# Sigmoid attention and two expert layers on one core: another order for the layer-1 weight work beside attention

## The chip, the core and the metric

The kernel runs on one core of one Trainium2 chip. The metric is device time in microseconds (us) of one execution. Engines are named as in the profile: PE is TensorE (matmuls), PEld its weight loads, DVE VectorE, ACT ScalarE, POOL GpSimd and SP SyncE, which here issues the DMAs.

## What is computed

```
scores = q @ k.T / sqrt(64) - log(448)              # 4 batches, 12 heads, 448 tokens, head size 64
x  = sigmoid(scores) @ v                            # heads side by side: 1792 tokens x 768
h  = x @ w1_in ;  x2 = (h * cos(h)) @ w1_out        # 768 -> 2048 -> 768
h  = x2 @ w2_in
P  = a0 + a1 h + a2 h^2 + a3 h^3
Q  = 1 + |b0| |h| + |b1| h^2
out = (P / (Q + 1e-6)) @ w2_out                     # 768 -> 2048 -> 768
```

The inputs are double precision. The weights reach the chip as pairs of 32-bit words; q, k and v as float32.

## The kernel before

**Products.** A matmul of the expert layers is three f16 products: the scaled operand is split into a high half (`hi`, written by ACT) and the rest (`lo`, written by DVE), and hi*hi, hi*lo and lo*hi are summed. So every weight row block needs a power-of-two scale, which comes from the row's largest magnitude, and every batch of activations needs a scale that comes from a maximum over the batch.

**Attention** fills the first 167 us. It goes by 24 pairs of heads in 84 units `(p, c)`; a unit is one chunk of 128 keys of a pair, and units `(p, None)` take the remaining 64 keys of two pairs together. For a unit, `scores` (L278) writes a tile `s_p_c` in the PSUM pool `pss` (2 tiles), ACT makes the sigmoid `a_p_c` (L280), and `av` (L296) adds its product with v to the PSUM tiles `v_p`. The k and q of a pair are first split into `kh`, `qh` (ACT, L256) and `kl`, `ql` (DVE, L257). When two pairs are complete, `av_out` copies each `v_p` to `raw_p` (ACT, L305) and then takes its maxima into `mx_x` (DVE, L308). The tiles `v_p` come from the PSUM pool `psa` of 4 tiles. All other PSUM tiles of this stage come from the same four: the `px_...` tiles of a maximum over partitions, and the first two products of layer 1, `h0` and `h1`. A tile is handed to the next user in the order in which tiles become free.

**Weight work beside attention.** DVE and ACT prepare layer-1 weights at the same time. There are 18 cells of `w1_in` (row block `r`, column piece `n`) and 2 cells of `w1_out` (`EARLY`). A cell is a load of word pairs `f1i_r_n` or `f1o_f` by SP into one of three buffers (L109), then on DVE `p0` (L78), `p1` (L81), a maximum (L113) and `p2` (L81), which write the value tile `v1i` or `v1o`. Behind a row block, `fin` works out its scale (tiles `re_...`, `s1i`, `i1i`), and then its pieces are split, `hi` on ACT (L343) and `lo` on DVE (L81). The other 14 row blocks of `w1_out` get only their maxima now (`max_cell`): a load `p1o_f` into the same three buffers, and one DVE reduction (L113). Whenever `p2` or such a maximum is through with its buffer, `prefetch` issues the next load of the list.

**Scales of x.** For batch `bt`, `x_begin(bt)` multiplies maxima and weight scales (`mxs_x`), reduces them and spreads the result over a diagonal `dg_x` (three DVE instructions). `xtwo(bt)` is a matmul of ones with it (`px_x`, L101) on PE, and on DVE a reduction `xm_x` and five small instructions that end in the scales `kx_x`. `x_split(0, d)` writes the f16 halves of x for batch 0. `t1_one` and `t1_two` do the same over all scales of `w1_out` (`dg_t`, `px_t`, `rho`, `irho`, `kap`).

**What sets the order.** The instructions of each engine run in the order in which the code emits them. All weight steps and scale steps stand in a list `work`, each with a cost. For every two units `slot()` is called three times; it hands out steps until their cost reaches the same share of the whole as the calls have, and a step with a third element 1 ends the call. The order within the loop is: scores of two units, k and q splits, a slot, `av` of the two units before, `av_out` if due, two slots. After the loop stand `l1_consts(0)`, the 18 matmuls of `h0`, the last `av` and `av_out`, then `h1`. From `h1` on, layer 1 and layer 2 run on PE to the end.

**Before**, `work` is the 20 cells in order with a maximum behind every cell from the fifth on, then batch 0's scale steps and x splits among the last cells, then `t1_one`, two empty steps, `t1_two`, `x_begin(1)`, `x_begin(2)`, `xtwo(1)`, `xtwo(2)`.

## Time and profile before

| | us |
|---|---|
| median of 3 runs | 1055.4 |
| the runs | 1055.65, 1055.4, 1054.65 |
| the profiled execution, its own time | 1054.34 |
| its span in the trace | 1052.4 |
| PE busy | 1030.3 (98%) |
| DVE busy | 806.4 (77%) |
| ACT busy | 575.0 (55%) |
| POOL busy | 212.9 (20%) |

The shares are means over stages with different limits: attention with its weight work lasts to 167.46, where `h1` begins; layer 1 and layer 2 fill the rest. The mean granted TensorE clock over the span is 0.993 of full speed.

### The profile page before, as it was taken

The page shows a single profiled execution, that of the slowest core. Times are in us where ns is not written, and L with a number is a line of the kernel's source. Part 1 is how long each engine was busy: PE and PEld are TensorE (multiplying, and loading weights), DVE is VectorE, ACT ScalarE, POOL GpSimd, SP SyncE. Part 2 cuts the span into 40 slices and gives each one's busy share as a digit, 9 for nine tenths or more (in the row PEclk, how much of TensorE's full clock was granted, in tenths as well). Part 3 has the DMA queues.
Part 4 walks back from the last instruction along what each step waited for, and adds up shares of the span by engine and source line. Part 5 has one row for each costly group of instructions (what it writes and reads, how often), then busy time and mean ns, then how long its engine had stood idle before and what let it go on. Part 6 is the DMA issues. An engine that isn't in the chain of part 4 may idle for free.

```text
span 1052.4 us, 15806 instructions
## 1 busy us (share of the span) xinstructions
PE 1030.3 (98%) x5920; PEld 550.0 (52%) x5920; DVE 806.4 (77%) x1541; ACT 575.0 (55%) x938; POOL 212.9 (20%) x211
## 2 busy tenths in 40 slices
PE   8999899999999999999999998989999999999998
PEld 5444444555555555555555554545565555555665
DVE  5999967877997799869996869888887873887200
ACT  6899886743474327532662555666665653666100
POOL 0000003766242004200240323312221110221000
PEclk9999999999999999999999999999999999999999
DMA  8899813224433562335437330000000000000000
GB/s 290 301 330 338 324 52 106 91 81 140 138 91 111 176 214 81 98 114 159 128 99 284 116 107 1 1 1 9 16 23 16 8 23 16 8 12 13 24 23 31
DMA packets 53485, 110.34 MB, mean 105 GB/s; under 512 B 5280, under 2 KB 29344, under 8 KB 52640
## 3 DMA queue, kind: packets, MB, share of 16 engines
q1 hardware_dynamic: 53408, 109.34, 31.4%
q8 instruction: 46, 0.75, 0.3%
q14 instruction: 31, 0.25, 0.1%
HBM read 91.23 MB, written 18.09 MB: 104 GB/s over the span
## 4 chain that ended last, share of the span: by engine, by line
PE 83%; DVE 8%; ACT 3%; DMA 3%; issue 1%; SPq 0%; DVEq 0%; ACTq 0%
PE hx L539 21%; PE o L614 21%; PE o L920 20%; PE hy L539 16%; PE v L296 3%; PE s L278 2%; DMA f1i<-in_moe_w_in_dram 1%; DVE w L81 1%; DVE t L81 1%; DVE v1i L81 1%; DMA k<-in_k_dram 1%; ACT a L280 1%; DMA f1o<-in_moe_w_out_dram 1%; PE s_None L278 1%; DVE kl L257 1%
## 5 line engine op out<-in xcount | busy, mean ns | idle before, releaser
L539 PEld LDWEIGHTS <-wi 128*128 128x128 f16 x2304 | 226.1, 98 | 212.1 <-issue 4.5
L920 PE MATMUL o<-wo,g 128*128 128x384 f16 (+1 forms) x1536 | 221.9, 326 | 4.1 <-ACT g L143 2.9
L539 PE MATMUL hy<-y,wi 128*128 128x448 f16 x1152 | 224.3, 355 | 0.0
L614 PE MATMUL o<-g,wo 128*128 128x448 f16 x1152 | 220.5, 352 | 0.0
L539 PE MATMUL hx<-x,wi 128*128 128x448 f16 x1152 | 218.7, 352 | 0.2 <-DVE xm_x L102 0.2
L920 PEld LDWEIGHTS <-g 128*128 128x128 f16 (+1 forms) x1536 | 134.2, 101 | 90.2 <-ACT g L143 3.2
L614 PEld LDWEIGHTS <-wo 128*128 128x128 f16 x1152 | 112.7, 98 | 104.3
L78 POOL TENSOR_SCALAR w<-u,aab 128x448 f32<-128x448 f32 x64 | 66.0, 1031 | 334.6 <-ACT u L883 321.2
L588 POOL TENSOR_TENSOR g<-r,g 128x448 f16<-128x448 f32 x64 | 73.1, 1145 | 233.6 <-ACT g L587 230.3
L280 ACT ACTIVATE a<-s,nlogs 128x896 f32<-128x896 f32 x72 | 69.2, 1005 | 16.9 <-PE s L278 16.8
L143 ACT ACTIVATE g<-t,kn 128x448 f16<-128x448 f32 x64 | 42.8, 669 | 54.5 <-DVE t L81 48.1
L894 ACT ACTIVATE u<-w,c 128x448 f32<-128x448 f32 x64 | 42.6, 665 | 52.0 <-DVE w L889 50.5
L81 DVE SCALAR_TENSOR_TENSOR w<-w,c,u 128x448 f32<-128x448 f32 x64 | 43.7, 683 | 31.1 <-ACT u L895 30.3
L575 ACT ACTIVATE k<-hx,quarter,ck 128x448 int32<-128x448 f32 x64 | 45.7, 714 | 36.4 <-PE hx L539 18.9
L78 POOL TENSOR_SCALAR xs<-v1o,s1o 128x384 f32<-128x384 f32 x28 | 26.5, 948 | 188.4 <-DVE v1o L81 186.9
L296 PE MATMUL v<-a,v 128*64 128x448 f32 x288 | 64.2, 560 | 0.0
L883 ACT ACTIVATE u<-hy,i_y 128x448 f32<-128x448 f32 x64 | 39.7, 620 | 36.0 <-PE hy L539 36.0
L887 DVE TENSOR_TENSOR t<-t,h 128x448 f32<-128x448 f32 x64 | 43.8, 685 | 20.2 <-ACT t L885 20.2
L81 DVE SCALAR_TENSOR_TENSOR t<-t,ab,w 128x448 f32<-128x448 f32 x64 | 56.9, 890 | 2.3
L76 DVE TENSOR_SCALAR ob<-o,ig 128x384 f32<-128x384 f32 x12 | 7.4, 614 | 64.4 <-PE o L920 64.4
L81 DVE SCALAR_TENSOR_TENSOR r<-hx,ck,k 128x448 f32<-128x448 f32 x64 | 43.4, 678 | 14.6 <-ACT k L575 14.5
L81 DVE SCALAR_TENSOR_TENSOR r<-hx,kap,r 128x448 f32<-128x448 f32 x64 | 43.3, 677 | 10.2 <-ACT r L581 10.0
(157 smaller groups left out, 1273.0 us busy)
## 6 DMA issues: line engine op xcount, KB each, us to landing
f2o<-in_moe_w_out_dram SPq DMA_DIRECT2D x32, 384.0 KB, 3.3
p1o<-in_moe_w_out_dram SPq DMA_DIRECT2D x14, 768.0 KB, 5.7
f1o<-in_moe_w_out_dram SPq DMA_DIRECT2D x28, 384.0 KB, 3.4
f1i<-in_moe_w_in_dram SPq DMA_DIRECT2D x12, 768.0 KB, 6.8
f2i<-in_moe_w_in_dram SPq DMA_DIRECT2D x24, 384.0 KB, 3.4
k<-in_k_dram SPq DMA_DIRECT2D x24, 256.0 KB, 4.9
wso<-hlo SPq DMA_DIRECT2D x32, 192.0 KB, 2.3
wi<-wsi SPq DMA_DIRECT2D x6, 1024.0 KB, 10.7
```

The source lines that it names most:

```text
L78: eng.tensor_scalar(out=o, in0=i, scalar1=s1, scalar2=s2, op0=op0, op1=op1)
L81: eng.scalar_tensor_tensor(out=o, in0=i0, scalar=s, in1=i1, op0=op0, op1=op1)
L143: A.activation(out=hi, in_=x, func=AF.Copy, scale=s)
L280: A.activation(out=t, in_=ps[:, :, :S], func=AF.Sigmoid, bias=cst["nlogs"], scale=QK)
L296: T.matmul(pvt[2 * o + j][h * D:(h + 1) * D, :S], vt[r, b * D:(b + 1) * D], at[r, x], start=c == (None if i else 0), stop=c == (NC - 1 if ...
L539: T.matmul(ps[:, :S], w[:, wl, f * P:(f + 1) * P], x[:, xl, :], start=(n == 0), stop=(n == 3 * ND - 1),)
L575: A.activation(out=kk, in_=ps[:, :S], func=AF.Identity, scale=ck, bias=cst["quarter"])
L588: G.tensor_tensor(out=g[:, 1, :], in0=r, in1=g[:, 0, :], op=ALU.subtract)
L614: T.matmul(acc[e][:, :S], w[:, wl, e * P:(e + 1) * P], g[:, gl, :], start=(f == 0 and i == 0), stop=(f == NF - 1 and i == 2),)
L887: V.tensor_tensor(out=t, in0=t, in1=h, op=ALU.mult)
L894: A.activation(out=u, in_=w, func=AF.Abs_reciprocal_sqrt, bias=cst["c1"])
L920: T.matmul(ps[o:o + m, :HALF], gt[bt, f][:, gl, c0:c0 + m], wo[f][:, wl, n0:n0 + HALF], start=(n == 0), stop=(n == 3 * NF - 1),)
```

## The change

The steps are the same, and each engine has as many instructions as before; their order is another.

- At the start one load of weights is issued ahead of the first parameters instead of three; the second follows k and q of pair 2, the third the second v.
- In the 18 cells of `w1_in`, a maximum of `w1_out` follows only every second cell from the eighth on (6 of 14). The other 8 stand in a list of 13 last steps, one behind each as long as there are any.
- Those last steps hold the scale steps of batches 0, 1 and 2 and the six x splits, in the order of `tail`; a step that is due brings a cell or a split of weights with it. `xtwo(0)` now comes three entries after `x_begin(0)`.
- `t1_two` and `l1_consts(0)` stand behind `h0` and the last `av_out`, ahead of `h1`.
- `kx` has three buffers instead of two.

```diff
--- before.py
+++ after.py
@@ -153,7 +153,7 @@
     SEAM = 2
     ESPLIT = 3
     NW = 3
-    WN, XN = 2, 7
+    XM, XN = 6, 7
     W_IN = [(c0, HALF) for c0 in range(0, 4 * HALF, HALF)] + [(4 * HALF, 256), (4 * HALF + 256, 256)]
     W_OUT = pieces(DM, HALF)
     W_BIG = [(0, DM), (DM, DM), (2 * DM, DFF - 2 * DM)]
@@ -182,7 +182,7 @@
             shr(e, m, 23)
             setexp(s, e, -1.0, 267)
             setexp(i, e, 1.0, -13)
-            kx = col(f"kx_{pfx}{bt}", ND, tag="kx", bufs=2)
+            kx = col(f"kx_{pfx}{bt}", ND, tag="kx", bufs=3)
             ts(V, kx, i_in, s)
             res[bt] = (e, s, i, kx)
 
@@ -414,35 +414,54 @@
             add_w1i(r)
         for f in range(EARLY):
             add_w1o(f)
-        x0 = [(0.5, lambda: x_begin(0)), (0.1, lambda: None), (1.0, lambda: xtwo[0]())]
-        x0 += [(0.75, lambda d=d: x_split(0, d)) for d in range(ND)]
         maxes = [max_cell(f) for f in range(EARLY, NF)]
-        splits = []
-        n_in = ND * len(W_BIG)
-        held = None
-        for n, ((ld, p0, p1, mx, p2), _) in enumerate(cells):
+        splits, held = [], []
+
+        def add_cell(n):
+            (ld, p0, p1, mx, p2), _ = cells[n]
             loads.append(ld)
-            work += [p0, held, p1, mx, p2] if held else [p0, p1, mx, p2]
-            held = None
+            work.extend([p0, *held, p1, mx, p2])
+            held.clear()
             if splits:
-                (hi, held), splits = splits[0], splits[1:]
+                hi, lo = splits.pop(0)
                 work.append((0.0, hi))
-            if len(maxes) * (len(cells) - 4) > (NF - EARLY) * (len(cells) - 1 - n):
+                held.append(lo)
+            if n in after:
+                fin, mine = after[n]
+                work.append(fin)
+                splits.extend(cells[i][1] for i in mine)
+
+        def add_max():
+            if maxes:
                 ld, mx = maxes.pop(0)
                 loads.append(ld)
                 work.append(mx)
-            if n in after:
-                fin, mine = after[n]
-                work.append(fin)
-                splits += [cells[i][1] for i in mine]
-            if n >= n_in and x0:
-                for _ in range(3):
-                    if x0:
-                        work.append(x0.pop(0) + (1,))
-        for hi, lo in splits:
-            work += [(0.0, hi), held, (0.0, lambda: None, 1)]
-            held = lo
-        work += [held] + [u + (1,) for u in x0]
+
+        n_in = ND * len(W_BIG)
+        for n in range(n_in):
+            add_cell(n)
+            if n >= XM and n % 2:
+                add_max()
+        xb, xg, xs = (
+            lambda bt: (0.5, lambda: x_begin(bt)), lambda bt: (1.0, lambda: xtwo[bt]()),
+            lambda d: (0.75, lambda: x_split(0, d)),
+        )
+        tail = [xb(0), xb(1), None, xg(0), xs(0), xg(1), xs(1), xs(2), xb(2), xs(3), xs(4), xg(2), xs(5)]
+        nexts = list(range(n_in, len(cells)))
+        for u in tail:
+            if nexts:
+                add_cell(nexts.pop(0))
+            elif splits:
+                hi, lo = splits.pop(0)
+                work.extend([(0.0, hi), *held])
+                held[:] = [lo]
+            else:
+                work.extend(held)
+                held.clear()
+            add_max()
+            if u:
+                work.append(u + (1,))
+        assert not (maxes or splits or held or nexts)
         st1 = {}
 
         def t1_one():
@@ -461,10 +480,7 @@
             ts(V, kap1, i1o, rho)
 
         rho, irho, kap1 = col("rho"), col("irho"), col("kap1", NF)
-        nop = lambda: None
-        work += [(0.7, t1_one, 1), *[(0.1, nop, 1)] * WN, (0.9, t1_two, 1)]
-        work += [(0.5, lambda bt=bt: x_begin(bt), 1) for bt in range(1, B - 1)]
-        work += [(1.0, lambda bt=bt: xtwo[bt](), 1) for bt in range(1, B - 1)]
+        work += [(0.7, t1_one, 1)]
         total = sum(u[0] for u in work)
         SLOTS = 3 * len(units) // 2 - 2
         clock = [0, 0.0]
@@ -485,15 +501,16 @@
             T.matmul(warm[:, :P], ones.to_broadcast([P, P]), ones.to_broadcast([P, P]), start=True, stop=True)
         A.activation(out=ab[:, :1], in_=ones, func=AF.Sigmoid)
         load_v(0)
-        for _ in range(NF64[0]):
-            prefetch()
+        prefetch()
         SY.dma_start(ab[:, 0:4], a.partition_broadcast(P))
         SY.dma_start(ab[:, 4:6], b.partition_broadcast(P))
         steps = prep(0)
         for st in "kh qh kl ql".split():
             steps[st]()
         load_kq(2)
+        prefetch()
         load_v(1)
+        prefetch()
         done = []
         for g in range(0, len(units), 2):
             due = [1] if g == 0 else []
@@ -550,12 +567,13 @@
             V.tensor_tensor(out=iy, in0=i, in1=irho, op=ALU.mult)
             return ck, iy
 
-        L1c = {0: l1_consts(0)}
         h0 = h_matmul("x", 0, 0)
         for p, c in units[-2:]:
             av(p, c)
         av_out(NP - 2)
         av_out(NP - 1)
+        t1_two()
+        L1c = {0: l1_consts(0)}
         h1 = h_matmul("x", 0, 1)
         pa.close()
         bp = ctx.enter_context(tc.tile_pool(name="pb", bufs=1, reuse_waits="tile"))
```

SP's queue from the first weight load on. Each row is one DMA; `f1i_0_1` is the second column piece of row block 0 of `w1_in`, `k_2` the k of pair 2. Before:

```order
L109 DMA f1i_0_0_123<-in_moe_w_in_dram 128x1536
L109 DMA f1i_0_1_125<-in_moe_w_in_dram 128x1536
L109 DMA f1i_0_2_127<-in_moe_w_in_dram 128x1024
L490 DMA ab_87<-in_moe2_a_dram 128x4
L491 DMA ab_87<-in_moe2_b_dram 128x2
L238 DMA k_2_139<-in_k_dram 128x512
L238 DMA q_2_141<-in_q_dram 128x448
L244 DMA v_1_143<-in_v_dram 128x896
```

After:

```order
L109 DMA f1i_0_0_123<-in_moe_w_in_dram 128x1536
L505 DMA ab_87<-in_moe2_a_dram 128x4
L506 DMA ab_87<-in_moe2_b_dram 128x2
L238 DMA k_2_135<-in_k_dram 128x512
L238 DMA q_2_137<-in_q_dram 128x448
L109 DMA f1i_0_1_139<-in_moe_w_in_dram 128x1536
L244 DMA v_1_141<-in_v_dram 128x896
L109 DMA f1i_0_2_143<-in_moe_w_in_dram 128x1024
```

The second and third weight loads moved behind `k_2` and `q_2`, the third behind `v_1` too.

PE's queue around `px_x0`, the matmul with batch 0's maxima. In the names a number behind the tile is its pair and chunk, the last one only a running number. Before:

```order
L278 MATMUL s_19_2_1514<-qh_19_1397,kh_19_1395 128x448 x2
L278 MATMUL s_19_2_1514<-qh_19_1397,kl_19_1396 128x448 x2
L278 MATMUL s_19_2_1514<-ql_19_1398,kh_19_1395 128x448 x2
L101 MATMUL px_x0_1535<-dg_x0_1501,ones_71 128x128
L296 MATMUL v_18_1443<-a_18_None_1463,v_9_1295 64x448
L296 MATMUL v_19_1444<-a_18_None_1463,v_9_1295 64x448
L296 MATMUL v_18_1443<-a_18_None_1463,v_9_1295 64x448
L296 MATMUL v_19_1444<-a_18_None_1463,v_9_1295 64x448
L296 MATMUL v_18_1443<-a_19_0_1472,v_9_1295 64x448
```

After:

```order
L101 MATMUL px_x0_1590<-dg_x0_1418,ones_71 128x128
L278 MATMUL s_20_2_1604<-qh_20_1479,kh_20_1477 128x448 x2
L278 MATMUL s_20_2_1604<-qh_20_1479,kl_20_1478 128x448 x2
L278 MATMUL s_20_2_1604<-ql_20_1480,kh_20_1477 128x448 x2
L278 MATMUL s_20_None_1613<-qh_20_1479,kh_20_1477 128x448
L278 MATMUL s_20_None_1613<-qh_21_1533,kh_21_1531 128x448
L278 MATMUL s_20_None_1613<-qh_20_1479,kl_20_1478 128x448
L278 MATMUL s_20_None_1613<-qh_21_1533,kl_21_1532 128x448
L278 MATMUL s_20_None_1613<-ql_20_1480,kh_20_1477 128x448
L278 MATMUL s_20_None_1613<-ql_21_1534,kh_21_1531 128x448
L296 MATMUL v_20_1630<-a_20_0_1563,v_10_1456 64x448
L296 MATMUL v_21_1631<-a_20_0_1563,v_10_1456 64x448
```

`px_x0` moved behind the last `av` of pair 19 (16 rows later in PE's queue). The second matmul of pair 20's `av`, into `v_21`, comes 11 rows behind it; its PSUM tile was freed by `xm_x0`, the reader of `px_x0`, before; after the change it is the one that the maxima `mx_x3` of `v_18` free.

DVE's queue up to those maxima of `v_18` and `v_19`. Before (`dg_x0`, which `px_x0` reads, stands three rows above the first of these, `m1o<-p1o_15` ten above):

```order
L102 TENSOR_REDUCE xm_x0_1499<-px_x0_1535 128x1
L76 TENSOR_SCALAR xm_x0_1499<-xm_x0_1499 128x1
L76 TENSOR_SCALAR e_x0_1538<-xm_x0_1499 128x1
L78 TENSOR_SCALAR s_x0_1539<-e_x0_1538 128x1
L78 TENSOR_SCALAR i_x0_1540<-e_x0_1538 128x1
L76 TENSOR_SCALAR kx_x0_1545<-i1i_84,s_x0_1539 128x6
L78 TENSOR_SCALAR v1o_1_1553<-f1o_1_1375 128x768
L81 SCALAR_TENSOR_TENSOR wi1_5_1413<-v1i_5_0_1180,s1i_97,wi1_5_1413 128x768
L81 SCALAR_TENSOR_TENSOR v1o_1_1553<-f1o_1_1375,v1o_1_1553 128x768
L113 TENSOR_REDUCE m1o_81<-f1o_1_1375 128x1
L308 TENSOR_REDUCE mx_x3_1582<-v_18_1443 128x1
L308 TENSOR_REDUCE mx_x3_1582<-v_19_1444 128x1
```

After (`dg_x0` stands 14 rows above the first of these, `xm_x0` is the row behind the last):

```order
L113 TENSOR_REDUCE m1o_81<-p1o_9_1369 128x1
L171 TENSOR_TENSOR mxs_x1_1506<-mx_x1_729,i1i_84 128x6
L96 TENSOR_REDUCE pm_x1_1510<-mxs_x1_1506 128x1
L76 TENSOR_SCALAR dg_x1_1509<-ident_66,pm_x1_1510 128x128
L257 TENSOR_TENSOR kl_21_1532<-k_21_1402,kh_21_1531 128x512
L257 TENSOR_TENSOR ql_21_1534<-q_21_1404,qh_21_1533 128x448
L81 SCALAR_TENSOR_TENSOR wi1_5_1299<-v1i_5_1_1175,s1i_97,wi1_5_1299 128x768
L113 TENSOR_REDUCE m1o_81<-p1o_10_1409 128x1
L81 SCALAR_TENSOR_TENSOR wi1_5_1299<-v1i_5_2_1254,s1i_97,wi1_5_1299 128x512
L113 TENSOR_REDUCE m1o_81<-p1o_11_1490 128x1
L308 TENSOR_REDUCE mx_x3_1583<-v_18_1446 128x1
L308 TENSOR_REDUCE mx_x3_1583<-v_19_1447 128x1
```

The maxima of `v_18` have the same number of rows ahead of them. Among these, `p1o_12` to `p1o_15` and the `xm_x0` chain are no longer there; the last `p2` of `v1o_1`, its scale, two `lo` pieces of `wi1_5` and `x_begin(1)` are.

PE's queue between the last `av` and `h1`. Before:

```order
L296 MATMUL v_22_1728<-a_23_1_1792,v_11_1587 64x448
L296 MATMUL v_23_1729<-a_23_1_1792,v_11_1587 64x448
L296 MATMUL v_22_1728<-a_23_2_1801,v_11_1587 64x448
L296 MATMUL v_23_1729<-a_23_2_1801,v_11_1587 64x448
L539 LDWEIGHTS wi1_0_297
L539 MATMUL hx_0_1_1873<-x0_0_1623,wi1_0_297 128x448
```

After:

```order
L296 MATMUL v_22_1738<-a_23_1_1805,v_11_1588 64x448
L296 MATMUL v_23_1739<-a_23_1_1805,v_11_1588 64x448
L296 MATMUL v_22_1738<-a_23_2_1814,v_11_1588 64x448
L296 MATMUL v_23_1739<-a_23_2_1814,v_11_1588 64x448
L101 MATMUL px_t1_1861<-dg_t1_1822,ones_71 128x128
L556 LDWEIGHTS wi1_0_297
L556 MATMUL hx_0_1_1873<-x0_0_1639,wi1_0_297 128x448
```

`px_t1` moved here from among the last scores. `h1` took the PSUM tile of `px_x2` before; now it takes that of `v_22`, which `mx_x3` of `v_22` frees.

## Rows read from the trace of the kernel before

**Rows 1.** Busy time by stretch: stretch, length, busy of each engine, PEclk, DMA share, GB/s.

```profile
16.00:125.80 109.80, 107.25 (x664) 52.04 (x664) 106.68 (x183) 98.67 (x136) 0.00 (x0) 1.00 0.90 322
...
130.40:136.00 5.60, 5.60 (x24) 2.43 (x26) 5.09 (x12) 0.00 (x0) 0.00 (x0) 0.52 0.30 99
...
167.50:628.50 461.00, 461.00 (x2444) 239.40 (x2443) 381.14 (x789) 226.98 (x391) 139.33 (x134) 1.00 0.42 133
```

**Rows 2.** SyncE timeline, start: start, us, what, count of issues.

```profile
3.06 1.92 SPq L109 DMA_DIRECT2D f1i<-in_moe_w_in_dram  x3
```

**Rows 3.** Chain of waits, first 60 us: start, us, piece of the chain.

```profile
6.22 9.06 DMA k<-in_k_dram
...
22.32 1.65 PE v L296 x8
23.97 1.42 PE s_None L278 x6
...
27.84 1.41 PE s L278 x12
29.25 1.81 PE v L296 x12
```

**Rows 4.** VectorE timeline, `kl` of pair 2: start, us, instruction [idle before].

```profile
16.03 0.69 DVE L257 TENSOR_TENSOR kl<-k,kh 128x512 fp32r<-128x512 f32 x1 [2.36 <-ACT kh L256]
```

**Rows 5.** TensorE timeline, scores behind the gap of the start.

```profile
17.48 0.47 PE L278 MATMUL s<-qh,kh 64*128 64x448 f32 x2 [1.58 <-ACT a L280]
```

**Rows 6.** TensorE timeline, one product of pair 16.

```profile
104.50 0.47 PE L278 MATMUL s<-ql,kh 64*128 64x448 f32 x2
```

**Rows 7.** VectorE timeline, the `ql` that this product reads.

```profile
103.83 0.62 DVE L257 TENSOR_TENSOR ql<-q,qh 128x448 fp32r<-128x448 f32 x1
```

**Rows 8.** TensorE timeline, around `px_x0`.

```profile
130.37 0.80 PE L101 MATMUL px_x<-dg_x,ones 128*128 128x128 f32 x2 [4.56 <-DVE dg_x L76]
131.09 1.77 PE L296 MATMUL v<-a_None,v 64*64 64x448 f32 x8
...
136.49 1.72 PE L296 MATMUL v<-a,v 128*64 128x448 f32 x8
```

**Rows 9.** VectorE timeline, around `px_x0`.

```profile
129.57 0.15 DVE L171 TENSOR_TENSOR mxs_x<-mx_x,i1i 128x6 f32<-128x6 f32 x1
...
130.22 0.68 DVE L257 TENSOR_TENSOR kl<-k,kh 128x512 fp32r<-128x512 f32 x1
...
131.36 0.28 DVE L102 TENSOR_REDUCE xm_x<-px_x 128x1 f32<-128x128 f32 x1
...
132.38 0.55 DVE L78 TENSOR_SCALAR v1o<-f1o 128x768 int32<-128x768 int32 x1
132.85 1.01 DVE L81 SCALAR_TENSOR_TENSOR wi<-v1i,s1i,wi 128x768 f16<-128x768 f32 x1
133.78 0.95 DVE L81 SCALAR_TENSOR_TENSOR v1o<-f1o,v1o 128x768 int32<-128x768 int32 x1
134.65 0.94 DVE L113 TENSOR_REDUCE m1o<-f1o 128x1 f32<-128x768 f32 x1
```

**Rows 10.** Who waited for whom, VectorE, 9 to 162 us: us in total, times, longest.

```profile
DVE v1i L78 <- DMA f1i<-in_moe_w_in_dram: 1.8, 2, 1.6
```

**Rows 11.** TensorE timeline, last units of attention.

```profile
153.38 0.67 PE L278 MATMUL s_None<-qh,kh 128*128 128x448 f32 x2 [1.29 <-ACT a L280]
...
161.44 0.71 PE L101 MATMUL px_x<-dg_x,ones 128*128 128x128 f32 x4
162.31 3.56 PE L539 MATMUL hx<-x,wi 128*128 128x448 f16 x18 [0.16 <-DVE xm_x L102]
165.80 1.72 PE L296 MATMUL v<-a,v 128*64 128x448 f32 x8
167.46 4.71 PE L539 MATMUL hx<-x,wi 128*128 128x448 f16 x24
```

**Rows 12.** VectorE timeline, last maxima of attention.

```profile
168.13 1.16 DVE L308 TENSOR_REDUCE mx_x<-v 128x1 f32<-128x448 f32 x2 [3.90 <-ACT raw L305]
```

**Rows 13.** Page, DMA issues: tile, count, KB, median us from issue to landing.

```profile
p1o<-in_moe_w_out_dram SPq DMA_DIRECT2D x14, 768.0 KB, 5.7
```

## The prediction

> **What bounds the kernel now.** I read the busy time by stretch first. From 167.5 to 628.5 PE is busy for 461.00 of 461.00 us [rows 1]. The change leaves the order behind `h1` as it is, so all that it can move is the moment at which `h1` starts, 167.46 [rows 11]. In the stretch before, 16 to 125.8, PE is busy for 107.25 and DVE for 106.68 of 109.8 us [rows 1]. Two such numbers don't say who waits, so I read the timelines of both at one place. The `ql` that begins at 103.83 and lasts 0.62 ends at 104.45, and the product that reads it starts at 104.50 [rows 6, 7]. PE takes the `ql` the moment DVE has it: DVE is the pace-maker, and PE can't be further along than DVE lets it.
>
> Then the two large gaps. The first is at the start. `k_2` is issued behind three loads of weights that were sent together from 3.06 on [rows 2], and lands 9.06 us after its issue at 6.22 [rows 3]. DVE therefore idles 2.36 us ahead of `kl` at 16.03 [rows 4], and PE 1.58 us ahead of the scores at 17.48 [rows 5]. The second is `px_x0`. PE has nothing for 4.56 us until `dg_x0` is there, at 130.37 [rows 8], because DVE reaches `dg_x0` only then [rows 9]. Behind this the granted clock is 0.52 from 130.4 to 136.0 [rows 1], the lower of the two levels (1.2 of 2.4 GHz). Its price: from 130.37 to 136.49 [rows 8] PE does one `px`, one `av` of 12 matmuls and one pair of scores. At full speed these are 0.36 (0.71 for two) [rows 11], 1.81 and 1.41 [rows 3], 3.58 together, and they took 6.12. So the low clock cost 2.54 us, and the whole place 7.1 us.
>
> **The change, part by part.** I follow DVE to one mark, the maximum `mx_x3` of `v_18`, then PE from there to `h1`.
>
> *DVE to the mark.* In the kernel before, DVE is through with the work ahead of it at 134.65 + 0.87 = 135.52; then it waits. 0.87 us is the step from one instruction of this width to the next, 133.78 to 134.65 [rows 9]. After the change four maxima of `w1_out` (4 x 0.87) and the `xm_x0` chain (131.36 to 132.38, 1.02) no longer stand ahead: 4.50 out. In come one `p2` (0.87), four small scale instructions (0.50, an estimate from the six of the chain), two `lo` pieces (0.93, from 132.85 to 133.78, and 0.66, an estimate by width) and `x_begin(1)` (129.57 to 130.22, 0.65) [rows 9]: 3.61. The maximum itself ends 0.58 after its start (two take 1.16) [rows 12]. So the mark would be at 135.52 - 4.50 + 3.61 + 0.58 = 135.2, with the waits of before.
>
> *The start.* `k_2` now has one load of weights ahead of it. I take its 2.36 us as gone. What covers it: the two delayed loads are needed only when DVE has worked through the first column piece. If that cover fails, the wait moves from `kl` to `v1i` and nothing is won; the bounds are 0 and -2.36.
>
> *Loads in between.* DVE waited 1.8 us for `f1i` [rows 10]. With a maximum behind every second cell instead of every cell, a load has more DVE work ahead of it per buffer, and the traffic of eight maxima (768 KB each) leaves a stretch whose DMA share is 0.90 [rows 1]. Bounds 0 and -1.8; I take -1.2, since the loads then lead by about one maximum more. The mark is at 135.2 - 2.4 - 1.2 = 131.6, between 131.0 and 135.2.
>
> *`px_x0`.* `dg_x0` now stands 24 DVE rows ahead of the mark and `px_x0` 11 PE rows ahead of `v_21`, so the 4.56 us go, and the 2.54 us with them. What is late next is new: the second matmul of pair 20's `av`, into `v_21`, has to wait for the mark, as it takes the PSUM tile of `v_18`. Queued behind it on PE is everything to the end. When would PE be there by itself? The scores ahead of `px_x0` ended at 130.37 - 4.56 = 125.81. To `v_21` PE now has 1.81 + 1.41 + 1.65 + 0.36 + 2.13 (one unit of 1.42 and half a pair of 1.41) + 0.41 (a quarter of 1.65) = 7.77 [rows 3, 11], which gives 133.58; less the 1.58 of the start, 132.0 at the latest, and earlier by what DVE's pace takes from it now. So both roads meet at 131.6 to 132.0, and I take 131.7. The wait of PE at `v_21` itself lies between nothing and 4 us; about 2 is likeliest, since DVE sets the pace up to there (between its `ql_21` and the mark stand 0.93 + 0.87 + 0.66 + 0.87 + 0.58 = 3.9 us of DVE work, and PE has some 1.5 left to do behind that `ql_21`).
>
> *From the mark to `h1`.* PE: the rest of that `av` 1.24; scores 1.41; `av` 1.81; `px_x1` 0.36; scores 1.41; `av` 1.65; scores 1.41; `av` 1.65; 2.13; `av` 1.65; `px_x2` 0.36; scores 1.41; `av` 1.81; `h0` 3.49 (162.31 to 165.80); `av` 1.65: 23.44 [rows 3, 11]. DVE has some 12 us of work in these first 15 (counted below) and keeps ahead of it, even with eight maxima and three scale chains. ACT held PE up by 1.29 at 153.38 [rows 11]; the x splits that stood side by side ahead of that `a` now stand one by one, so I let that go (bounds 0 and +1.3). `h1` then waits for the maximum of `v_22`: last `av` done at 167.46 [rows 11], `mx_x` starts at 168.13 and its first half ends 0.58 later [rows 12]. That is 1.25 us, with `px_t1` inside it, where before there was no wait. `l1_consts(0)` behind it costs nothing: what reads it comes after ACT's copies of the same `v`. The third `kx` buffer and the dropped empty steps are no work.
>
> **Sum.** `h1` at 131.7 + 23.44 + 1.25 = 156.4, which is 11.1 us earlier than 167.46. The profiled execution took 1054.34, so 1043.3; it lies 1.06 below the median of 1055.4, on whose scale the forecast is **1044.4 us**. Own range 1042.6 to 1046: down by the last 0.6 of the loads and the 1.25 of `h1`, up by ACT's 1.3 and small waits.
>
> **Rivals.** *The clock falls again.* The gaps of 1.58 and 1.29 us [rows 5, 11] left the clock at full speed (1.00 over 16 to 125.8), the one of 4.56 did not [rows 1, 8]; a wait of 2 to 4 us at `v_21` lies between them. The same units as before stand behind such a gap, so I price it at the same 2.54: 1046.9. The Trainium skill (TensorE: Matmul & The Clock Gate, section "A second HAM failure mode: psum-queue depth-cycling") tells of a kernel in which short idles between matmul groups that wait for PSUM brought the throttle back. By that the new wait for a PSUM tile would lose the clock; no row here shows it for a gap under 4.56.
>
> *The start does not do what it says.* Small loads are issued behind one big one all the same, and DVE then waits for `f1i_0_1`. That keeps 2.4 us, and up to 1.2 more if the later loads wait as before: 1046.8 to 1048.
>
> *More than that.* If no load is waited for and the maximum of `v_22` is ready by the end of `px_t1`, 1.4 us less: under 1042.6.
>
> *Slower than before.* The eight late maxima share three buffers. The load of `p1o_12` is issued when the maximum of `p1o_9` is through, that of `p1o_15` when `p1o_12` is. From `p1o_9` to the mark DVE has 0.65 + 1.14 (`kl` and `ql`, 130.22 to 131.36) + 0.93 + 0.87 + 0.66 + 0.87 + 0.58 = 5.7 us of work, and from there to `p1o_15` another 10.5: the second maximum 0.58, two scale chains 2.04, two `lo` 1.86, twice `kl` and `ql` 2.28, three maxima 2.61, two x halves of 0.6 [rows 9, 12]. Two landings plus 0.87 each must fit into these 16.2 us. With the median of 5.7 [rows 13] they take 13.1 and fit; with 9.06, as `k_2` had it [rows 3], 19.9, and `h1` is up to 3.7 later. Above a landing of 12.8 us, (16.2 + 11.1) / 2 - 0.87, the whole gain is lost, 1055.4 and more. Against it: most of them fall where the DMAs had little to do.
>
> **How the numbers follow.** Chances: forecast 0.56, clock 0.16, start 0.14, more 0.07, slower or nothing won 0.07. The range from 1041.5 to 1048.5 holds the first three and part of the fourth; what is left out is the rest of that and the last. 0.2% (2.1 us) is about what a measurement of this kernel can tell from no change: faster means under 1053.3. Forecast, clock, start and more are all faster, and 0.01 of the last case (a loss of 3.7 from long landings stays faster too): 0.94. Within 0.2%: 0.02, slower 0.04.
>
> **What would show it.** Right: `h1` near 156.4; no gap at `px_x0`; `kl` of pair 2 without an idle of 2 us before it; a gap at `v<-a` near 130 that ends with `mx_x`; about 0.8 us ahead of `h1` behind `px_t`; a granted clock of 1.00 throughout. A clock near 0.5 behind the gap is the first rival; DVE waits for `f1i` of 2 us near 11 to 18 the second; DVE waits for `p1o` of over 3 us in the tail the last. I am wrong in kind if anything behind `h1` changes its length by more than 1 us.

## The result, and the profile after

The changed kernel takes 1042.94 us (median of 4 runs, 1042.32 to 1043.68) against 1055.53 (4 runs): a ratio of 0.988, with a 95% interval from 0.9865 to 0.9894. A second set of 4 runs beside 7 of the kernel before gave 1042.78 against 1055.65, ratio 0.9876 (0.986 to 0.9893). So it is faster by 12.6 to 12.9 us; forecast were 11.0, and 1044.4 within 1041.5 to 1048.5.

Where layer 1 starts is read from PE's timeline. Of the changed kernel: start, us, instruction, and in brackets the idle time before it and what ended it.

```profile
14.96 0.47 PE L278 MATMUL s<-qh,kh 64*128 64x448 f32 x2
...
125.06 0.49 PE L101 MATMUL px_x<-dg_x,ones 128*128 128x128 f32 x2
...
127.72 0.96 PE L296 MATMUL v<-a,v 128*64 128x448 f32 x2
129.87 1.72 PE L296 MATMUL v<-a,v 128*64 128x448 f32 x6 [1.19 <-DVE mx_x L308]
131.52 0.47 PE L278 MATMUL s<-qh,kh 64*128 64x448 f32 x2
...
154.01 0.49 PE L101 MATMUL px_t<-dg_t,ones 128*128 128x128 f32 x2
155.36 4.89 PE L556 MATMUL hx<-x,wi 128*128 128x448 f16 x25 [0.86 <-DVE mx_x L308]
```

`h1` starts at 155.36 instead of 167.46 [rows 11], 12.1 us earlier; a second profile of the changed kernel has it at 156.16. The scores behind the gap of the start come at 14.96 instead of 17.48 [rows 5] with no idle time before them; `px_x0`, which had 4.56 us of it [rows 8], has none. Two new waits stand there as forecast: 1.19 us at `v_21` for the maximum of `v_18`, and 0.86 us ahead of `h1` for that of `v_22`. From 9 us to `v_21` PE has no gap of 0.1 us or more: up to there it no longer waits for VectorE.

VectorE of the changed kernel, the same two moments and the loads.

```profile
10.14 0.56 DVE L78 TENSOR_SCALAR v1i<-f1i 128x768 int32<-128x768 int32 x1 [0.54 <-DMA f1i<-in_moe_w_in_dram]
...
13.34 0.68 DVE L257 TENSOR_TENSOR kl<-k,kh 128x512 fp32r<-128x512 f32 x1
...
128.34 0.95 DVE L113 TENSOR_REDUCE m1o<-p1o 128x1 f32<-128x768 f32 x1 [0.18 <-DMA p1o<-in_moe_w_out_dram]
129.21 1.14 DVE L308 TENSOR_REDUCE mx_x<-v 128x1 f32<-128x448 f32 x2
```

`kl` of pair 2 starts at 13.34 instead of 16.03 [rows 4] and waits for nothing. The 1.8 us for `f1i` [rows 10] are gone; 0.54 and 0.18 are all that is left of waits for loads up to the mark. The maximum of `v_18` starts at 129.21 and, by half of the pair, ends at 129.79.

Busy time by stretch of the changed kernel (columns as in [rows 1]), then the stretch from 60 to 90 of the kernel before and, last, of the changed one.

```profile
16.00:118.00 102.00, 102.00 (x644) 50.32 (x642) 101.10 (x183) 94.72 (x130) 0.00 (x0) 1.00 0.87 306
...
125.00:131.00 6.00, 4.81 (x23) 2.50 (x22) 5.72 (x12) 5.65 (x9) 0.00 (x0) 1.00 0.90 330
131.00:157.00 26.00, 25.14 (x151) 11.96 (x150) 18.16 (x51) 15.78 (x23) 0.00 (x0) 1.00 0.40 139
```

```profile
60.00:90.00 30.00, 30.00 (x190) 14.46 (x186) 29.68 (x53) 27.45 (x39) 0.00 (x0) 1.00 0.94 337
```

```profile
60.00:90.00 30.00, 30.00 (x196) 14.77 (x196) 29.79 (x53) 27.59 (x38) 0.00 (x0) 1.00 0.84 295
```

PE is full, 102.00 of 102.00, where it was 107.25 of 109.8 [rows 1], and the clock stays at 1.00 throughout. The eight late maxima lower the DMA share of the middle from 0.94 to 0.84; that of the tail, 131 to 157, rises from 0.17 to 0.40.

### The profile page after: what moved, and what is told of

Same layout as the page of the kernel before. It is cut to its first block, busy times and chain, and to the rows that moved or that the text cites. A ratio compares the mean times of both kernels' runs of the same rounds, so it can differ in the third digit from the quotient of the medians.

```text
span 1041.6 us, 15803 instructions
## 1 busy us (share of the span) xinstructions
PE 1027.0 (99%) x5920; PEld 549.5 (53%) x5920; DVE 806.1 (77%) x1541; ACT 575.0 (55%) x938; POOL 213.6 (21%) x211
## 4 chain that ended last, share of the span: by engine, by line
PE 91%; DVE 5%; ACT 2%; issue 1%; DMA 1%; POOL 0%; DVEq 0%; ACTq 0%; POOLq 0%
PE hx L556 21%; PE o L632 21%; PE o L938 20%; PE hy L556 17%; PE v L296 6%; PE s L278 4%; DVE w L81 1%; DVE t L81 1%; PE s_None L278 1%; DMA p1o<-in_moe_w_out_dram 1%; ACT u L912 0%; ACT u L913 0%; PE warm L501 0%; ACT y L143 0%; DVE m1o L113 0%
```

## The experiments

Each is read by the start of `h1`: whole times also hold what differs behind `h1` from one execution to the next (last section). Ahead of `h1` executions differ too: the two profiles of the changed kernel have it 0.8 us apart. Where that matters, the distance from the mark (the start of the maximum of `v_18`) to `h1` is given, which lies inside one execution. The times given are single runs unless said otherwise.

### The start, undone and alone

In the changed kernel, the old start:

```diff
         load_v(0)
-        prefetch()
+        for _ in range(NF64[0]):
+            prefetch()
...
         load_kq(2)
-        prefetch()
         load_v(1)
-        prefetch()
```

> The changed kernel with the three loads of weights of the start sent together again, as before the change. Theory (VectorE sets the pace up to the maximum mx_x3 of v_18): VectorE idles some 2.4 us ahead of kl of pair 2 again, the wait of 0.54 us for the first f1i goes, and layer 1 starts (h1) 1.8 to 2.4 us later than the 155.4 of the changed kernel, near 157.5. Rival (the start is made up for in the long stretch behind it, where TensorE is full): h1 within 0.7 us of 155.4.

`h1` at 158.94, 3.6 us later than in the first profile of the changed kernel, 2.8 later than in the second (1045.47 us in all). And the kernel before with only the new start, the same lines the other way:

> The kernel before with only the start of the changed kernel: one load of weights ahead of k_2 and q_2. Theory: VectorE is 2.4 us earlier at dg_x0 and so is px_x0; h1 at 165.0 to 165.7 instead of 167.46, the gap at px_x0 stays at 3.5 to 4.6 us and the clock still falls behind it. Rival (the gap at px_x0 takes the gain up): h1 within 0.7 us of 167.5, the gap longer by what TensorE gains.

`h1` at 164.44, 3.0 us earlier (1052.74 against 1054.1 of the kernel before, run beside it). VectorE's rows of the first of the two, then the busy time of a stretch of it:

```profile
16.02 0.69 DVE L257 TENSOR_TENSOR kl<-k,kh 128x512 fp32r<-128x512 f32 x1 [2.45 <-ACT kh L256]
...
29.49 0.69 DVE L257 TENSOR_TENSOR kl<-k,kh 128x512 fp32r<-128x512 f32 x1 [0.24 <-ACT kh L256]
...
69.60 0.69 DVE L257 TENSOR_TENSOR kl<-k,kh 128x512 fp32r<-128x512 f32 x1 [0.25 <-ACT kh L256]
...
131.88 0.98 DVE L113 TENSOR_REDUCE m1o<-p1o 128x1 f32<-128x768 f32 x1 [0.37 <-DMA p1o<-in_moe_w_out_dram]
```

```profile
18.30:21.70 3.40, 3.37 (x14) 1.60 (x14) 3.37 (x6) 2.77 (x5) 0.00 (x0) 0.50 0.59 193
```

The start carries through to `h1`; the rival that it is made up for falls. Both runs move `h1` by more than their theories said (1.8 to 2.4 us, and 165.0 at the earliest), and not all of that belongs to the start.

In the first run, `kl` of pair 2 starts at 16.02, for 13.34 and 13.86 in the two profiles of the changed kernel, and behind it come three small waits of 0.24, 0.25 and 0.37. PE's idle time ahead of the scores of pair 2 is 2.18 us in this execution, and behind it the clock falls: granted 0.50 from 18.3 to 21.7, so that two units of scores and an `av` take 4.90 us (17.49 to 22.39). In the kernel before, where the same idle time is 1.58 [rows 5], they take 3.36 at full clock. Whether the wait of 0.24 for `kh` follows from this is not shown.

In the second run the gap at `px_x0` stayed, at 4.70 us (expected were 3.5 to 4.6): VectorE is late there, and PE came earlier too. `px_x0` stands at 127.86 instead of 130.37, 2.5 us earlier. The other 0.5 us goes with a shorter stretch of work at half clock behind it: 4.3 us (to 132.15) instead of 5.4 (to 135.78).

### `px_x0` alone

In the kernel before, only `px_x0` and its reader are moved:

```diff
-        x0 = [(0.5, lambda: x_begin(0)), (0.1, lambda: None), (1.0, lambda: xtwo[0]())]
+        x0 = [(0.5, lambda: x_begin(0)), (0.1, lambda: None), (1.0, lambda: None)]
...
                 av_out(p)
+                if p == 19:
+                    xtwo[0]()
```

> The kernel before with only px_x0 and its reader xm_x0 moved behind the maxima of v_18 and v_19 (dg_x0 stays). Rival (the gap at px_x0 is a loss of its own): 4.6 us of gap and 2.5 us of half clock both go, h1 at 160.4. Theory (behind that gap VectorE's work up to the mark is late next): the gap at px_x0 goes and the clock stays full, but TensorE then waits 1 to 2 us at the second matmul into v_21 until the maximum of v_18, which VectorE can't reach before 135; v_21 5.7 us earlier than the 140.8 of before, h1 at 161.4 to 162.3.

`h1` at 161.97, 5.5 us earlier (1049.25). PE's rows:

```profile
131.51 0.49 PE L101 MATMUL px_x<-dg_x,ones 128*128 128x128 f32 x2
...
134.15 0.97 PE L296 MATMUL v<-a,v 128*64 128x448 f32 x2
135.67 1.72 PE L296 MATMUL v<-a,v 128*64 128x448 f32 x6 [0.55 <-DVE mx_x L308]
```

Gap and half clock at `px_x0`, 7.1 us together, both go, and 1.5 us of this come back at once, because PE now waits at `v_21` for the maximum of `v_18`. Only 0.55 of it is idle time, less than the 1 to 2 expected; the other 0.97 is the first matmul of the `av`, which now runs alone while the rest takes as long as the whole did. `h1` is where I expected it. This run lost the clock at another place, though: behind an idle time of 1.77 us at 17.26, ahead of the scores of pair 2, the granted clock is 0.50 from 18.8 to 22.1, which the kernel before does not have. So 5.5 us may be somewhat too little for `px_x0`. Removing a gap is worth its length less what the engine behind it is late with.

Both parts in one kernel:

> The kernel before with the new start and the late px_x0 together: the two parts that took 3.0 and 5.5 us off h1 alone. Theory (both act on the same chain, VectorE's work up to the maximum of v_18, and add up): h1 at 158.5 to 159.5, so that 3.1 to 4.1 us of the changed kernel's gain are left for the place of the maxima and the order of the tail. Rival (they overlap): h1 at 160.5 or later.

`h1` at 158.44, 9.0 us earlier (1045.67): 3.0 and 5.5 add up to 8.5, and the other 0.5 is no more than executions differ by at the start (`kl` of pair 2 at 12.96 here, at 13.47 in the run with the start alone). That leaves 3.1 of the 12.1 us, or 2.3 by the second profile, for the place of the maxima and the order of the tail. Of this, 0.8 us lies behind the mark: from there (131.49) to `h1` are 26.95 us here, 26.15 with the change. Among them is PE's wait of 1.13 us for ACT at 144.37, which the changed kernel no longer has. No run has the order of the tail by itself.

### The place of the maxima

```diff
             add_cell(n)
-            if n >= XM and n % 2:
+            if n >= 4:
                 add_max()
```

> The changed kernel with a maximum of w1_out behind every one of the w1_in cells from the fifth on (all 14 done there), none in the tail. Theory (VectorE has the same sum of work to the end of attention, only the waits for loads differ): up to 2 us of waits for f1i come back, h1 at 155.4 to 157.5. Rival (it is the maxima in the tail that make room): 4 us or more later than 155.4.

`h1` at 163.37, 8.0 us later than with the change (1051.3). My theory falls, the rival holds. Who VectorE waited for, from 8 to 150 us (us in total, times, longest):

```profile
DVE v1i L78 <- DMA f1i<-in_moe_w_in_dram: 5.8, 8, 1.7
DVE kl L257 <- ACT kh L256: 4.6, 2, 3.1
DVE v1o L78 <- DMA f1o<-in_moe_w_out_dram: 1.0, 1, 1.0
```

6.8 us of waits for loads instead of 0.7. (Of the second line, 3.1 stand at 8.5 us, in the changed kernel too, and 1.5 at 146, behind the mark.) The work is the same to the instruction; 14 cells in a row now each bring a load of 768 or 512 KB and one of 768 KB, and DVE outruns them. The mark is 6.9 us later (136.09 instead of 129.21). The other 1.1 come behind it: steps are handed out by cost, so that `px_x0` now falls behind the first `av` of pair 20 and waits there for the maximum of `v_18`, 1.10 us. The kernel before spread its 14 maxima over 16 cells and was held up by its start, so this run says that the room must be there, not how much the kernel before lost by it. That smaller part is bounded by the run with both parts: its waits for loads are 1.44, 0.53 and 0.47, 2.4 us in all.

### The wait for `v_18`: longer and shorter

Three or six reductions over 448 columns more ahead of the maximum of `v_18`; nothing else reads them:

```diff
+        spare = col("spare")
...
                 p = done.pop(0)
+                if p == 18:
+                    for _ in range(3):
+                        V.tensor_reduce(out=spare, in_=raw[1, 0], axis=AX, op=ALU.max)
                 av_out(p)
```

> The changed kernel with three reductions over 448 columns more on VectorE (0.53 us each) just ahead of the maximum of v_18. Theory: TensorE's wait at v_21 grows from 1.2 to 2.8 us, the clock stays full, h1 1.6 us later, at 157.0. Rival (a wait of this length loses the clock): half clock for some units behind it, h1 4 us later, at 159.5. Rival (VectorE doesn't set this moment): h1 within 0.5 us of 155.4.

> The changed kernel with six such reductions: TensorE's wait at v_21 grows to 4.4 us, about as long as that at px_x0 before the change (4.56). Theory (a wait of this length loses the clock whatever is waited for): granted clock near 0.5 behind it, h1 3.2 us later for the work and 2 to 2.5 for the clock, at 160.6 to 161.1. Rival (the clock at px_x0 fell for another reason): clock 1.00, h1 at 158.6.

With three, `h1` at 159.41 (1046.79); with six, at 161.10 (1048.34). PE of the first, then its stretches, then the row of the second, and last the maximum of `v_18` on VectorE, of the first and of the second:

```profile
132.31 2.85 PE L296 MATMUL v<-a,v 128*64 128x448 f32 x6 [2.59 <-DVE mx_x L308]
135.09 0.74 PE L278 MATMUL s<-qh,kh 64*128 64x448 f32 x2
```

```profile
130.00:132.00 2.00, 0.00 (x0) 0.00 (x0) 1.93 (x4) 1.69 (x3) 0.00 (x0) 1.00 1.05 411
132.00:134.00 2.00, 1.69 (x5) 0.63 (x6) 1.90 (x9) 0.14 (x1) 0.00 (x0) 0.69 0.99 411
134.00:136.00 2.00, 2.00 (x6) 0.83 (x6) 2.00 (x4) 0.52 (x1) 0.00 (x0) 0.50 1.00 412
136.00:138.00 2.00, 2.00 (x18) 0.95 (x18) 2.00 (x3) 1.44 (x2) 0.00 (x0) 0.96 0.41 109
```

```profile
133.51 3.25 PE L296 MATMUL v<-a,v 128*64 128x448 f32 x6 [4.52 <-DVE mx_x L308]
```

```profile
131.65 1.15 DVE L308 TENSOR_REDUCE mx_x<-v 128x1 f32<-128x448 f32 x2
```

```profile
132.84 1.15 DVE L308 TENSOR_REDUCE mx_x<-v 128x1 f32<-128x448 f32 x2
```

A wait of 2.59 us at this place lost the clock: granted 0.50, that is 1.2 GHz, from about 133 to 136, and the six matmuls took 2.85 instead of 1.72. The theory that the clock holds through a wait of this length falls; the first rival holds.

What the clock costs is read from the mark to `h1`, since the executions reach the mark at different times. In the changed kernel this is 26.15 us (129.21 to 155.36; 26.16 in its second profile), with three reductions 27.76, with six 28.26. So the lost clock costs 1.6 and 2.1 us, not the 2.54 of the prediction. That is about half of the time that PE worked at half clock, 3.4 us (132.75 to 136.17) and 4.4 (133.51 to 137.95). The rest of the move of `h1` is the mark: the three reductions took 1.86 us and not 1.6, the six 3.82 and not 3.2, and the first of the two executions was 0.6 us late already when they began. That the sums of the expectations, 159.5 and 160.6 to 161.1, came out is in part luck.

The Trainium skill (TensorE: Matmul & The Clock Gate, section "A second HAM failure mode: psum-queue depth-cycling") tells of a kernel that cycles through PSUM, in which PE idles briefly and often between matmul groups and the throttle comes back by that. Here one wait for a PSUM tile was enough when it was 2.59 us long; that many short ones do it, no run here shows. The change stood nearer to this than I thought: 1.19 us at `v_21` kept the clock and 2.59 did not, and ahead of the scores of pair 2 1.58 kept it [rows 5] while 1.77 and 2.18 lost it. These are single executions; one and the same idle time can go either way (last section).

The other way, the maximum two VectorE instructions earlier:

```diff
+            hold = (19, 2) in units[g:g + 2] or (19, 2) in units[g - 2:g]
+            if not hold:
-            slot()
+                slot()
...
             slot()
             slot()
+            if hold and (19, 2) in units[g - 2:g]:
+                slot()
+                slot()
```

> The changed kernel with the maxima of v_18 and v_19 two VectorE instructions earlier: the last lo of wi1_5 and the maximum of p1o_11 (1.7 us with its wait) now stand behind them. Theory: TensorE's wait of 1.19 us at v_21 goes to below 0.1, and h1 is 1.0 to 1.2 us earlier, at 154.2 to 154.4, as VectorE has 0.8 us in hand in the tail. Rival (the tail of VectorE is late then): half of it or less, 154.8 or later.

`h1` at 154.49 (1041.23), and the maximum:

```profile
127.48 0.95 DVE L113 TENSOR_REDUCE m1o<-p1o 128x1 f32<-128x768 f32 x1
128.34 1.14 DVE L308 TENSOR_REDUCE mx_x<-v 128x1 f32<-128x448 f32 x2
```

The mark starts 0.87 us earlier (128.34 for 129.21), `h1` 0.87 earlier (154.49 for 155.36). That bears out the second part of the sum, a fixed way from the mark to `h1`: in both kernels `h1` stands 26.15 us behind the start of that maximum. The gain is a little under the 1.0 to 1.2 expected, since VectorE came to the splits of pair 21 later in this execution (`kl` at 125.42 for 124.48). The gap is gone from the timeline, yet the `av` there took 2.75 us instead of 1.65: 0.96 for its first matmul alone and 1.72 for the rest leave less than 0.1 of waiting. So the idle time of 1.19 is only about half of what this place costs the changed kernel:

```profile
127.98 2.75 PE L296 MATMUL v<-a,v 128*64 128x448 f32 x8
130.66 0.47 PE L278 MATMUL s<-qh,kh 64*128 64x448 f32 x2
```

### The wait ahead of `h1`

```diff
         h0 = h_matmul("x", 0, 0)
+        t1_two()
         for p, c in units[-2:]:
...
-        t1_two()
         L1c = {0: l1_consts(0)}
```

> The changed kernel with t1_two (px_t1 and its small instructions) between h0 and the last av instead of behind it. Theory (h1 waits for the maximum of v_22, whose PSUM tile it takes): h1 now takes the tile of px_t1, the wait of 0.86 us ahead of h1 goes, h1 at 154.5. Rival (the wait is for something else, such as ScalarE's copy of v_22): h1 still waits 0.5 us or more, at 155.0 or later.

`h1` at 154.31 (1041.86), with no idle time before it: the wait is for the PSUM tile, and with another tile it is gone. It is 1.05 us earlier, and from the mark (129.25) 25.06 us instead of 26.15, 1.09 less, for 0.9 expected.

### A faster version

Both of the last two edits together, beside the changed kernel once more on the same chip:

> The changed kernel once more, beside the next one on the same chip: 12 to 13 us below the kernel before. The granted clock behind the gap in layer 2, some 527 us behind h1, differs from one execution to the next, so single times should lie within about 1.4 us of each other with h1 at the same place.

> The changed kernel with the maxima of v_18 and v_19 two VectorE instructions earlier and t1_two between h0 and the last av: no gap at v_21 and none ahead of h1. Theory (the two waits are independent): h1 at 153.4 to 153.8, 1.5 to 2.0 us below the changed kernel. Rival (the tail of VectorE or ScalarE takes one of them back): 1.0 us or less.

1040.18 us (4 runs, 1038.98 to 1040.6) against 1042.78 (1041.75 to 1043.38), and 1055.65 before: ratio 0.9853 (0.9838 to 0.9868). `h1` at 153.31; PE is busy for 137.13 of the 137.30 us from 16 to there. The single times of the changed kernel lie 1.6 us apart, for 1.4 expected. The two waits are independent. The gain of 2.6 us is above the 1.5 to 2.0 expected, but part of it lies in how the executions began and ended (last section). Counted from the third unit of scores, which starts at 7.07 here and at 6.98 and 8.12 in the two profiles of the changed kernel, `h1` comes after 146.24 us instead of 148.38 and 148.04: 1.8 to 2.1 us less.

A last one put the maxima right behind the splits of pair 21 and `px_x2` behind `h0`:

```diff
-        tail = [xb(0), ... xs(4), xg(2), xs(5)]
+        tail = [xb(0), ... xs(4), None, xs(5)]
...
+            first, second = (19, 2) in units[g:g + 2], (19, 2) in units[g - 2:g]
+            if not first and not second:
-            slot()
+                slot()
...
-            slot()
-            slot()
+            for _ in range(0 if first else 6 if second else 2):
+                slot()
...
         h0 = h_matmul("x", 0, 0)
-        for p, c in units[-2:]:
-            av(p, c)
+        xtwo[2]()
+        av(*units[-2])
+        t1_two()
+        av(*units[-1])
...
-        t1_two()
```

> The version before this one, with the maxima of v_18 and v_19 right behind the splits of pair 21 on VectorE (four instructions earlier than in the changed kernel instead of two, x_begin(1) behind them as well), and px_x2 moved behind h0, since TensorE waited 0.17 us for its dg_x2 already. Theory (h1 follows the maximum of v_18 at a fixed distance of 25.6 us less the 0.9 us that h1 doesn't wait, until TensorE is full): the maximum ends near 127.3, the av into v_20 and v_21 takes 1.65 us again instead of 2.7, h1 at 152.0 to 152.6, about 1 us below the version before this one. Rival (VectorE's tail, with 1.7 us more work behind the mark, is late for the scores of pair 22 or for h0): h1 at 153 or later.

1040.95 us (4 runs, 1040.88 to 1041.12; before 1055.74, on another chip than the version before this one): no gain in the whole time. The maximum starts at 126.98, the `av` takes 1.72 again, and `h1` comes at 153.74, past the rival's 153, though not by its mechanism:

```profile
16.00:153.70 137.70, 137.70 (x862) 67.93 (x858) 131.25 (x255) 121.69 (x168) 0.00 (x0) 1.00 0.79 280
```

PE is full from 16 to `h1`, and there is no wait left to take. This execution began later: its third unit of scores starts at 8.22, in the version before at 7.07. From there to `h1` it takes 145.52 us, 0.7 less than the 146.24 of the version before, by one profile of each.

## Why the prediction was right

**The bound.** Right: all that the order moves is `h1`, and the time followed it.

**The start.** Right in mechanism and about right in size: 2.4 in the sum. Alone it brings `px_x0` forward by 2.5 us, and `kl` of pair 2 starts 2.2 to 2.7 earlier in the changed kernel than with the old start. The 3.0 and 3.6 us at `h1` hold more than that: a shorter stretch at half clock in the one, three small waits and an early start of the execution in the other.

**Loads in between.** Taken as -1.2 of 1.8. Behind `kl` of pair 2 all of it went, and 0.27 for `f1o` at 122.27 with it; 0.18 came. This term was about 0.7 too small.

**The mark.** Forecast at 131.6, found at 129.8 and, in the second profile, 130.6. In the first, 0.3 of the difference is the start, 0.7 the loads; the other 0.8 is VectorE's own way from `kl` of pair 2 to the mark, and no run shows where in it.

**`px_x0`.** Right: gap and half clock are gone, and late next is the maximum of `v_18`. The wait there was 1.19 (0.84 in the second profile), inside "nothing to 4", below the 2 taken. The reason given for 2, that VectorE sets the pace up to there, did not hold: PE has no idle time from 9 us to `v_20`, where it stood at 127.72, well before "132.0 at the latest". In the second profile its third unit of scores is 1.14 us later and `px_x0` 1.15, while the mark is 0.79 later. So the two reach `v_21` by separate roads, and the wait there is the difference of the two.

**From the mark to `h1`.** 24.7 in the sum, 25.6 measured (129.79 to 155.36). One term was mis-sized: I gave the rest of the split `av` three quarters of 1.65, 1.24. It took 1.65, since the first matmul of the four runs alone for 0.96 and the other six parts take as long as all eight. Three `px` of 0.42 instead of 0.36 are the next 0.2, and the rest is spread over small differences. The wait ahead of `h1`, foreseen as about 0.8, measured 0.86. ACT's wait of 1.29 is gone, as I had let it go.

**Sum.** `h1` forecast at 156.4, found at 155.36 and 156.16. In the first, the mark came 1.8 us earlier than in the sum and the way from it was 0.9 longer, so that the sum is nearer than its parts: that is luck. From one profiled execution to the other the time fell by 11.0 us, 1054.34 to 1043.37: 12.1 at `h1`, less some 1.3 that the changed one took longer behind it (last section). The 12.6 is larger because the profiled execution of before lies 1.19 under its median and that of the changed kernel 0.43 over its own.

**The rivals.** The clock stayed at 1.00, but a wait of 2.59 at the very place loses it: this danger was real, and its chance of 0.16 was not too high. Its price was: 2.54 forecast, 1.6 and 2.1 found, since PE worked at half clock for 3.4 and 4.4 us there, and for 5.4 us behind `px_x0` in the kernel before. The gap of 1.29 at 153.38 lies outside the stretch that the prediction names for it; from 150 to 158 the clock is 1.00 too. The start did what it says. The slower case needed landings of 12.8 us; the median of the `p1o` loads was 5.9, and the longest wait for one 0.18 us.

**"Wrong in kind if anything behind `h1` changes by more than 1 us."** In the profiles it did: 886.24 us from `h1` to the end against 884.94. The last section shows why that test was badly chosen.

**Not shown.** No run has the order of the tail, the third `kx` buffer or the place of `l1_consts(0)` by itself. That the last two cost nothing is argued, not shown.

## What to carry to other kernels

Follow the engine that sets the pace to the instruction at which the waiting engine next needs it, and from there the other engine to the end: a gap that goes is worth its length only up to the next such mark. When a matmul or its reader is moved, look at which PSUM tile each later tile now takes and who frees it; both waits that this change made, and the two edits that took them away again for 2.6 us, were of that kind. Work that only loads and reduces belongs where the DMAs have room; the same instructions, packed where they have none, cost 6.8 us of waits. And measure an effect between two marks inside one execution where you can: the moment at which single executions reach a mark differed here by up to 0.8 us, half of what a lost clock cost.

## What the runs showed of the hardware

**The same gap costs different amounts.** In layer 2, about 520 us behind `h1`, PE has a gap of some 4 us in every kernel, 2.9 of it for ScalarE's `g`. Stretches of 5 us behind it, first of the kernel before, then of the changed one:

```profile
687.46:692.46 5.00, 1.18 (x6) 0.24 (x4) 4.77 (x8) 2.94 (x6) 0.75 (x1) 0.97 0.02 5
692.46:697.46 5.00, 4.69 (x18) 2.14 (x19) 4.15 (x8) 3.27 (x6) 1.18 (x1) 0.69 0.00 0
697.46:702.46 5.00, 5.00 (x29) 2.57 (x27) 4.14 (x8) 3.58 (x6) 1.18 (x1) 1.00 0.00 0
```

```profile
675.36:680.36 5.00, 1.15 (x5) 0.21 (x3) 4.78 (x8) 2.94 (x6) 0.75 (x1) 0.95 0.02 5
680.36:685.36 5.00, 4.66 (x13) 1.94 (x14) 4.14 (x8) 3.30 (x6) 1.18 (x1) 0.50 0.00 0
685.36:690.36 5.00, 5.00 (x24) 2.46 (x23) 4.15 (x8) 3.58 (x6) 1.18 (x1) 0.87 0.00 0
```

The same instructions wait the same time, and the clock comes back earlier in one execution (0.69, then 1.00) than in the other (0.50, then 0.87). Over the 14 profiles of all these kernels the time behind `h1` lies between 884.76 and 886.36 us, with kernels of either order at both ends. In six of them the granted clock is 0.50 for 3.4 us at this gap, as in the first, and they have 884.76 to 885.36; in eight it is so for 6.8 us, and they have 885.44 to 886.36. The second profile of the changed kernel, word for word the same program, has 885.44 and its `h1` at 156.16: the first scores also begin earlier or later, by how soon the clock of the twenty warming matmuls rises (3.91 and 4.64 us for them). The third unit of scores starts between 6.98 and 8.22 in the 14 profiles. So up to 1.2 us ahead of `h1` and 1.6 behind it are no effect of an order.

**Two matmuls of an `av` step run side by side.** In the `av` of the changed kernel at 136.6, the first parts of the two start at 136.596 and 136.603. Eight parts take 1.65 us from start to start; when only the first matmul can go, its two parts take 0.96, and the six that follow take 1.65 (the rows of `v<-a,v` above). Holding back one of the pair therefore costs nearly 1 us here even when no idle time shows.

**The length of an idle time alone did not decide whether the clock was lost.** Ahead of `px_y` in layer 2, some 477 us behind `h1`, PE idles for 2.7 us in all 14 profiles. In eleven the granted clock behind it is 0.50, in three it stays at 1.00 (the start alone, the place of the maxima, and `t1_two` early). The row and the stretch of the changed kernel, then those of the run with the start alone:

```profile
632.61 0.77 PE L101 MATMUL px_y<-dg_y,ones 128*128 128x128 f32 x2 [2.70 <-ACT u L913]
```

```profile
632.60:635.40 2.80, 2.79 (x8) 1.42 (x9) 2.73 (x4) 1.55 (x3) 2.20 (x2) 0.50 0.00 0
```

```profile
641.69 0.46 PE L101 MATMUL px_y<-dg_y,ones 128*128 128x128 f32 x2 [2.68 <-ACT u L896]
```

```profile
641.70:645.10 3.40, 3.40 (x19) 1.93 (x20) 3.33 (x4) 1.53 (x3) 2.51 (x2) 1.00 0.00 0
```

Ahead of the scores of pair 2, 1.58 us kept the clock and 1.77 and 2.18 lost it; at `v_21`, 0.84 and 1.19 kept it and 2.59 and 4.52 lost it. Each of these is one execution, and what decides between them is not shown. The price in attention is about half of the time that PE then works at half clock: 1.6 us for 3.4, 2.1 us for 4.4, 2.54 for 5.4.
